# Attention and two mixtures of experts on one core: a new order for the first jobs of the second mixture, with earlier weight stores

## The chip, the cores and the metric

One core of one Trainium2 chip runs the whole program. The metric is device time in microseconds (us) of one execution, as the median of several runs.

## The reference, cut to what matters

```
kv  = einsum('bhsd,bhse->bhde', k, v);  out = einsum('bhsd,bhde->bhse', q, kv)   # q,k,v: 4 x 8 x 576 x 64
x   = out / sqrt(mean(out*out, -1) + 1e-6) * g_norm          # then 2304 rows of 512
p   = probs / (probs.sum(-1) + 1e-9)                         # first mixture, 4 experts, all of them
x1  = sum_e p[:, e] * (relu(x @ w1[e]) @ w2[e])              # 512 -> 1024 -> 512
logits = normed(x1) @ normed(emb).T / tau                    # second mixture, 8 experts
idx = argmax(logits);  gate = softmax(logits)[idx]
y[rows of e] = gate * (relu(x1[rows of e] @ w1b[e]) @ w2b[e])
```

Everything is float32.

## The kernel before, in words

Each float32 operand of a large product is split into a rounded high part and the rest (`split`, L60: the high part on ScalarE at L61, the low part on VectorE at L62), and each product is three TensorE products: high by high, high by low, low by high. The order of work on every engine is written out by hand. An engine executes its instructions in the order in which the Python code issues them, so where a call stands decides what it waits behind.

**Attention and the start.** Per batch and pair of heads, `kv_unit` (L120) forms k'v on TensorE and ScalarE copies it out. `x_unit`, `x_norm` and `xt_unit` (L186, L199, L221) form, normalise and transpose one tile of 128 rows; `x_norm` ends on VectorE at L202 and `xt_unit` transposes on TensorE at L225. The units of batch 1 read their k and v from memory that is later `en_b`.

**First mixture.** The rows go in units of 384. The first two units run four plain phases (`plain_phase`, L1143): four steps of the first layer (`plain_unit`, TensorE at L841), then six steps of the second (`l2_unit`, L948, two for each tile of 128 rows). A list `todo` hands side work out by a modelled time: `run_steps` issues an entry as soon as the sum of the steps' modelled times has passed the entry's. P1T = 8.4 is the end of a plain phase's first layer. The side work is, among other things, `w2_fills` (the split of two blocks of the second layer's weights into `w2h`, `w2l`, L1150), and `hold_now` (L77): it issues the stores that were put off, on the SyncE queue (SP, L69), which copy split weights to DRAM for later passes. Before, `hold_now` stands after all steps of the plain phase. The other units run phases with Strassen's scheme in 14 steps (TensorE at L853, ScalarE and VectorE sums at L860 and L864), with second-layer steps behind them (loop at L1196 on); `w2_fills(e, fh, 1, 6)` at L1200 spreads the two splits of w2 over the modelled times 1 to 6.

**Routing.** The last six tiles (t = 12 to 17) get their logits as products: after the tile's last `l2_unit`, an entry of `due` issues `logits_t` (L341, four transposes at L346, which read the tile `fin` that VectorE writes at L957) two ticks later and `logits_u` (L351) two more ticks on. A tick is one call of `background`, one per step. After the last tile the generator `route_b` (L533) is put into `bg`. It picks experts, counts places (`ranks`, L410, TensorE at L415), and inverts the places into lists of rows for the jobs (`invert`, L450: VectorE makes one-hot tiles `po` at L364, TensorE counts with them into `psi` at L476). `background` advances it by pieces; nearly all of them are small VectorE instructions. The first 12 tiles have been routed earlier (`route_a`), which gives the first NA = 5 jobs of 128 rows.

**Second mixture.** It runs jobs of one expert and 128 rows each. `gather` (L748, GpSimd) fetches a job's rows, `tx_unit` (L1118) transposes them on TensorE and splits them into `xgt` (high on ScalarE at L1123, low on VectorE, tile `xgl`, L360), `m1_unit` (L1234) is half of a first layer (12 steps of TensorE's L1240 per half of F, 24 per job), `th_unit` (L1248) transposes and splits half of its result, `m2_unit` (L1272) is a second layer (24 steps of L1262), `m2_out` (L1264) scales and scatters it. `slot_split` (L783) splits a job's weights; from job 2 on under a condition (`tc.If`, L791), because a job with the expert of two jobs earlier keeps its weights. `period` (L1290) pairs the first layer of job s with the second layer of job s - 1:

```
hn = m1_unit(s, 0), m1_unit(s, 1)
while (s + 2 >= NA and "placed" not in late): background(1)
ps = m2_unit(s - 1, ..., fill = tx_unit(s + 1), gather(s + 2))
th_unit(s, 0), th_unit(s, 1), m2_out(s - 1, ps)
```

For s = 0 there is no second layer, so the order is m1(0), tx_unit(1), th(0), m1(1). `tx_unit(1)` writes the same `xgt` that m1(0) reads. At s = 3 the rows of job 5 are gathered, which is the first gather that needs all of `route_b` (`placed`).

Of the kernel before, what the change touches and what calls it, by code (L numbers as in the profile page):

```python
# [20 lines left out]
def attn_moe_moe_kernel(ctx: ExitStack, tc: tile.TileContext, q, k, v, g_norm, dprobs, w1, w2, emb, tau, w1b, w2b, out):  # L21
    nc = tc.nc
# [277 lines left out]

    def inv_norm(a, shape, tag):
        pool = late.get("tmp", rt_p)
        b, r, y = (pool.tile(shape, F32, name=n, tag=n + tag) for n in ("inb", "inr", "iny"))
        nc.vector.tensor_scalar_max(b, a, 1e-30)
        nc.scalar.activation(out=r, in_=b, func=ACTF.Sqrt)
        twice_root(r, b, y)
        nc.vector.tensor_scalar(out=b, in0=r, scalar1=0.5, scalar2=1e-6, op0=ALU.mult, op1=ALU.add)
        nc.vector.reciprocal(b, b)
        return b

    def setup_emb():
# [29 lines left out]
    def logits_t(t, x):  # L341
        xx = late["tmp"].tile([128, NC, 128], F32, name="xx", tag="xx")
        due.append((tick[0] + (2 if t < NT - 1 else 1), t, lambda: logits_u(t, xx)))
        ps = psp.tile([128, NC, 128], F32, name="pslt", tag=f"x{t % 2}" if t < NT - 1 else nxt("l2"))
# [5 lines left out]

    def logits_u(t, xx):  # L351
        pl = psp.tile([128, E2], F32, name="psl", tag="kv")
        for c in range(NC):
            nc.tensor.matmul(out=pl, lhsT=xx[:, c], rhs=en_t[:, c], start=(c == 0), stop=(c == NC - 1))
        nc.vector.tensor_copy(lg[:, t], pl)
        if t == NT - 1:
            bg.append(route_b())
# [30 lines left out]

    def gate_exp(t0, t1, rx):
        l = lg[:, t0:t1]  # L390
        tt(l, l, bc(rx, [128, t1 - t0, E2], 2), ALU.mult)
        nc.scalar.activation(out=l, in_=l, func=ACTF.Exp)

# [96 lines left out]
    def route_a():  # L490
        rx = inv_norm(ssq[:, 0:TA], [128, TA], "a")
        yield from pick(0, TA)
        gate_exp(0, TA, rx)
        yield 1
# [37 lines left out]

    def route_b():  # L533
        rx = inv_norm(ssq[:, TA:NT], [128, NT - TA], "b")
        yield 0
        yield from pick(TA, NT)
        gate_exp(TA, NT, rx)
        yield 1
        ps, run = ranks(TA, NT)
        yield 0  # L540
        tab = tmp([128, E2], "tab")
        tt(tab, st_a, cnt, ALU.add)
        yield from places(TA, NT, ps, run, tab)
        gate_sum(TA, NT)
# [392 lines left out]
    def l2_unit(t, e, fh, part, i, first):  # L937
# [21 lines left out]
        if last:  # L959
            nc.gpsimd.dma_start(out=x1d[128 * t:128 * t + 128, :], in_=ac)  # L960
            if t < TA:
                bg.append(logits_v(t, ac))
            else:
                due.append((tick[0] + 2, t, lambda: logits_t(t, ac)))
            if t == TA - 1:
# [131 lines left out]
    for t in range(TS):  # L1097
        xt_unit(t, ("tp", "l10", "l11")[t], first=True)
    issue()
    def norm_probs():  # L1100
# [15 lines left out]
    xgt = []  # L1116

    def tx_unit(s):  # L1118
        xg = xgs.pop(s)
        ps = psp.tile([128, NC, 128], F32, name="pstx", tag="tp")  # L1120
        for c in range(NC):
            nc.tensor.transpose(ps[:, c], xg[:, 128 * c:128 * c + 128], ident)  # L1122
        nc.scalar.copy(xgt[0], ps)  # L1123
        tt(xgt[1], ps, xgt[0].bitcast(F32), ALU.subtract)

# [17 lines left out]
    def plain_phase(un, e, fh, todo, pace):  # L1143
        steps = [(P1T / 4, lambda f=f: plain_unit(un % 2, f)) for f in range(4)]
        steps += l2_steps(e, fh, [un], None, first_half, (P2T - P1T) / 6)
        run_steps(steps, todo, pace)
        if un == 0:
            hold_now()

# [13 lines left out]
    todo = w2_fills(0, 0) + [(-1, f) for f in plain_direct(1)]  # L1163
    todo += [(1.5 + 2 * p, lambda p=p: kv_unit(1, p)) for p in range(2, NP)] + [(6.0, norm_probs)]
    todo += [(10.0 + c, lambda c=c: nc.vector.tensor_tensor(
# [30 lines left out]
    for at_ph, ph in enumerate(strassen):  # L1196
        p, e, fh = ph
        steps = [(S1T / 14, f) for f in strassen_steps()]
        steps += l2_steps(e, fh, [2 * p, 2 * p + 1], (0, 1, 2, 0, 1, 3), lambda t: 0, (S2T - S1T) / 12)
        todo = w2_fills(e, fh, 1, 6) + ahead.get(ph, []) + carried + [(8.8, hold_now)]  # L1200
        carried = []
# [32 lines left out]
    def m1_unit(s, half, mid):  # L1234
        xh, xl = xgt
        ps = psp.tile([128, 512], F32, name="psm1", tag=nxt("l1"))
# [44 lines left out]
    def ahead_of(s):  # L1281
        if s + 1 < NS:
            tx_unit(s + 1)
        if s + 2 < NS:
            gather(s + 2)

    def idle():
        pass

    def period(s, mid1, mid2):  # L1290
# [3 lines left out]
        mid1()  # L1294
        while min(s + 2, NS - 1) >= known[0] or (s + 2 >= NA and "placed" not in late):
            background(1)
        if s:
            ps = m2_unit(s - 1, mid2, lambda: ahead_of(s))
        else:
            ahead_of(s)  # L1300
        th_unit(s, 0, hn[0])
        th_unit(s, 1, hn[1])
        if s:
            m2_out(s - 1, ps)

    def full_period(s):
        work2 = [lambda n=n: slot_split("w2", s, [n]) for n in range(4)]
        work1 = [lambda n=n: slot_split("w1", s + 1, [n]) for n in range(4 if s + 1 < NS else 0)]
        if s == 0:
            work1, work2 = work2, []  # L1310

        def side(work):
            if work:
                work.pop(0)()
            background(2 if s + 2 < NA else 1)

# [4 lines left out]

    for s in range(SURE):
        full_period(s)
# [50 lines left out]
```

## Time and profile before

| | |
|---|---|
| median of 3 runs | 1139.51 us (1139.37 to 1140.52) |
| the profiled execution | 1139.33 us |
| its span in the trace | 1137.5 us |
| TensorE busy | 1106.6 us, 97% of the span |
| VectorE busy | 629.6 us, 55% |
| ScalarE busy | 484.9 us, 43% |
| GpSimd busy | 190.1 us, 17% |

The span is the time between the first and the last instruction of the trace; the execution's own time is 1.8 us more. A time in a row is counted from the span's start. In a timeline, a row has the start, the duration, the engine (PE TensorE, ACT ScalarE, DVE VectorE, POOL GpSimd, SPq the issuing of transfers by SyncE), the line of the code, the operation, output<-inputs, shape and count, and in brackets how long the engine stood idle before and what ended that.

### The profile page before, as it was taken

What the parts mean: (1) busy time and instruction counts of PE and PEld (TensorE: products, weight loads), DVE (VectorE), ACT (ScalarE), POOL (GpSimd) and SP (SyncE); (2) the same over time, 40 slices, a digit from 0 to 9 for tenths busy, and PEclk for the clock granted to TensorE, in tenths of its full rate; (3) what the DMA queues carried; (4) which work ended last, traced back from release to release, by engine and by line L of the source; (5) the groups of instructions that cost most, each with busy time, mean ns of one, the idle gap of its engine ahead of it and who ended that gap; (6) DMA issues with size and microseconds to landing.
All of it is one profiled execution on the core that took longest, in us unless ns stands there. A gap on an engine that the chain in (4) does not pass through costs nothing. (4 is left out here: it accounts for less than half of the span.)

```text
span 1137.5 us, 17164 instructions
## 1 busy us (share of the span) xinstructions
PE 1106.6 (97%) x5894; PEld 970.7 (85%) x5894; DVE 629.6 (55%) x1187; ACT 484.9 (43%) x892; POOL 190.1 (17%) x232
## 2 busy tenths in 40 slices
PE   8989999999999999999999999999987999999997
PEld 7878898988888988899999988889876888888885
DVE  3555664666794456544573556643468573376362
ACT  3534446544454222233334222222464574475462
POOL 3101332313441100100120000010110112111211
PEclk9989999999999999999999999999999999999999
DMA  9645777766877455455465555445554583575571
GB/s 269 199 145 210 290 285 291 256 216 265 305 260 266 171 200 192 164 200 204 173 238 192 179 208 213 184 172 199 209 186 142 192 327 118 180 261 216 164 256 35
DMA packets 91011, 239.85 MB, mean 211 GB/s; under 512 B 19285, under 2 KB 38741, under 8 KB 90784
## 3 DMA queue, kind: packets, MB, share of 16 engines
q1 hardware_dynamic: 83472, 214.23, 53.2%
q0 software_dynamic: 7440, 24.41, 6.4%
q8 instruction: 49, 0.80, 0.3%
q14 instruction: 50, 0.41, 0.1%
HBM read 230.22 MB, written 56.63 MB: 252 GB/s over the span
## 5 line engine op out<-in xcount | busy, mean ns | idle before, releaser
L948 PE MATMUL bank<-w2h,hh 128*128 128x512 f32 x576 | 227.4, 395 | 0.2 <-ACT hh L825 0.2
L948 PE MATMUL bank<-w2l,hh 128*128 128x512 f32 x576 | 225.0, 391 | 0.1
L948 PE MATMUL bank<-w2h,hl 128*128 128x512 f32 x576 | 225.1, 391 | 0.0
L853 PE MATMUL bank<-xth,w1h 128*128 128x384 f32 x616 | 159.9, 340 | 2.5 <-ACT s L860 1.1
L853 PE MATMUL bank<-xtl,w1h 128*128 128x384 f32 x616 | 156.8, 335 | 0.0
L853 PE MATMUL bank<-xth,w1l 128*128 128x384 f32 x616 | 156.7, 335 | 0.0
L957 DVE SCALAR_TENSOR_TENSOR acc<-bank,dp,acc 128x512 f32<-128x512 f32 x120 | 89.8, 749 | 110.0 <-PE bank L948 109.8
L948 PEld LDWEIGHTS bank<-w2h,hl 128*128 128x128 f32 x576 | 108.2, 188 | 24.0 <-DVE hl L828 1.1
L948 PEld LDWEIGHTS bank<-w2h,hh 128*128 128x128 f32 x576 | 108.2, 188 | 22.4 <-ACT hh L825 1.4
L948 PEld LDWEIGHTS bank<-w2l,hh 128*128 128x128 f32 x576 | 108.2, 188 | 21.5 <-DMA w2l<-held_w 0.5
L853 PEld LDWEIGHTS bank<-xth,w1h 128*128 128x128 f32 x616 | 109.5, 188 | 6.7 <-ACT s L860 1.6
L62 DVE TENSOR_TENSOR w2l<-raw,w2h 128x1024 fp32r<-128x1024 f32 x64 | 76.7, 1220 | 64.0 <-ACT w2h L61 59.9
L853 PEld LDWEIGHTS bank<-xtl,w1h 128*128 128x128 f32 x616 | 111.5, 188 | 0.0
L853 PEld LDWEIGHTS bank<-xth,w1l 128*128 128x128 f32 x616 | 111.3, 188 | 0.0
L860 ACT COPY s<-bank 128x384 f32<-128x384 f32 x88 | 42.2, 479 | 157.6 <-PE bank L853 157.5
L864 POOL TENSOR_TENSOR sv<-sv,s 128x384 f32<-128x384 f32 x44 | 48.3, 1097 | 350.3 <-ACT sv L860 274.0
L336 DVE CUSTOM_DVE_ANT_0 scr<-row,en_b 128x512 bf16<-128x512 f32 x96 | 68.4, 713 | 13.4 <-DMA row<-x1d 8.6
L1262 PE MATMUL psy<-w2h,hth 128*128 128x512 f32 x176 | 72.2, 410 | 0.4 <-ACT hth L1253 0.4
L1262 PE MATMUL psy<-w2l,hth 128*128 128x512 f32 x176 | 69.8, 396 | 0.0
L1262 PE MATMUL psy<-w2h,htl 128*128 128x512 f32 x176 | 69.4, 394 | 0.0
L61 ACT CAST w2h<-raw 128x1024 fp32r<-128x1024 f32 x64 | 65.7, 1052 | 7.1 <-DMA raw<-in_moe_w_dram 2.8
L62 DVE TENSOR_TENSOR w1l<-raw,w1h 128x256 fp32r<-128x256 f32 (+2 forms) x75 | 55.3, 754 | 16.9 <-ACT w1h L61 16.5
(249 smaller groups left out, 1657.2 us busy)
## 6 DMA issues: line engine op xcount, KB each, us to landing
raw<-in_moe_w_dram SPq DMA_DIRECT2D x224, 512.0 KB
w1h<-held_w SPq DMA_DIRECT2D x28, 896.0 KB
w1l<-held_w SPq DMA_DIRECT2D x28, 896.0 KB
w2h<-held_w SPq DMA_DIRECT2D x34, 512.0 KB
w2l<-held_w SPq DMA_DIRECT2D x34, 512.0 KB
held_w<-w1h SPq DMA_DIRECT2D x16, 896.0 KB
held_w<-w1l SPq DMA_DIRECT2D x16, 896.0 KB
held_w<-w2h SPq DMA_DIRECT2D x16, 512.0 KB
```

Of the source, the lines that this page charges most:

```text
L61: nc.scalar.copy(hi, raw)
L62: (eng or nc.vector).tensor_tensor(out=lo, in0=raw, in1=hi.bitcast(F32), op=ALU.subtract)
L336: nc.vector.tensor_tensor_reduce(out=scr, in0=x, in1=en_b[:, e], scale=1.0, scalar=0.0, op0=ALU.mult, op1=ALU.add, accum_out=lg[:, t, e:e + 1]
L853: nc.tensor.matmul(out=ps, lhsT=wform(wo, b, w)[:, c], rhs=xform(xo, x)[:, c], start=start and n == 0, stop=(n == 5), skip_group_check=True)
L860: nc.scalar.copy(t, src)
L864: (eng or nc.vector).tensor_tensor(out=out, in0=a, in1=b, op=ALU.add)
L948: nc.tensor.matmul(out=ps, lhsT=h_t[o][f][u][:, ns], rhs=w[j][:, a], start=(k == 0 and m == 0), stop=(k == 3 and m == 2))
L957: nc.vector.scalar_tensor_tensor(out=fin, in0=ps, scalar=dp[:, t, e:e + 1], in1=ac, op0=ALU.mult, op1=ALU.add)
L1262: nc.tensor.matmul(out=ps, lhsT=x[:, f], rhs=w[j][:, o], start=(f == 0 and i == 0), stop=(f == NF - 1 and i == 2))
```

## The change

Seven edits. (1) The units of batch 1's pairs 2 and 3 are issued before the first plain phase and not at modelled times inside it. (2) In the plain phases of unit 0, `hold_now` is issued at P1T + 0.05, between the layers. (3) In the last phase of the first pass with Strassen's scheme, (0, 3, 1), the two splits of w2 are spread over 0.1 to 3.0. (4) `logits_t` comes one tick later for tiles 12 to 16; `logits_u` of tile 16 follows after one tick. (5) `inv_norm` is cut in two; in `route_b` its start comes with the last logits, its end and the products with it come after `ranks`, the exponential after that. (6) Job 1's x is split into the memory of the last w2 part of odd jobs, and the order becomes m1(0), m1(1), m2(0), with `tx_unit(1)` and `th_unit(0, ...)` inside the first layers; the weights of jobs 0 to 2 are split at new places; `route_b` goes forward by two pieces a tick in the first period and one from then on. (7) Job 5's gather, and the loop that finishes `route_b`, move behind job 2's second layer; that puts the products of `invert` into period 3, the fourth job.

```diff
@@ -298,15 +298,21 @@
-    def inv_norm(a, shape, tag):
+    def inv_start(a, shape, tag):
         pool = late.get("tmp", rt_p)
         b, r, y = (pool.tile(shape, F32, name=n, tag=n + tag) for n in ("inb", "inr", "iny"))
         nc.vector.tensor_scalar_max(b, a, 1e-30)
         nc.scalar.activation(out=r, in_=b, func=ACTF.Sqrt)
+        return b, r, y
+
+    def inv_end(b, r, y):
         twice_root(r, b, y)
         nc.vector.tensor_scalar(out=b, in0=r, scalar1=0.5, scalar2=1e-6, op0=ALU.mult, op1=ALU.add)
         nc.vector.reciprocal(b, b)
         return b
+
+    def inv_norm(a, shape, tag):
+        return inv_end(*inv_start(a, shape, tag))
@@ -340,7 +346,7 @@
     def logits_t(t, x):
         xx = late["tmp"].tile([128, NC, 128], F32, name="xx", tag="xx")
-        due.append((tick[0] + (2 if t < NT - 1 else 1), t, lambda: logits_u(t, xx)))
+        due.append((tick[0] + (2 if t < NT - 2 else 1), t, lambda: logits_u(t, xx)))
         ps = psp.tile([128, NC, 128], F32, name="pslt", tag=f"x{t % 2}" if t < NT - 1 else nxt("l2"))
         for c in range(NC):
             nc.tensor.transpose(ps[:, c], x[:, 128 * c:128 * c + 128], ident)
@@ -349,6 +355,8 @@
         nc.scalar.activation(out=sq.rearrange("p r n -> p (r n)"), in_=x, func=ACTF.Square, accum_out=ssq[:, t:t + 1])
     def logits_u(t, xx):
+        if t == NT - 1:
+            late["rx"] = inv_start(ssq[:, TA:NT], [128, NT - TA], "b")
         pl = psp.tile([128, E2], F32, name="psl", tag="kv")
         for c in range(NC):
             nc.tensor.matmul(out=pl, lhsT=xx[:, c], rhs=en_t[:, c], start=(c == 0), stop=(c == NC - 1))
@@ -386,9 +394,12 @@
         tt(oh[:, :, s].rearrange("p e t -> p t e"), a, bc(m2, sh, 2), ALU.is_equal)
         yield 1
-    def gate_exp(t0, t1, rx):
+    def gate_mul(t0, t1, rx):
         l = lg[:, t0:t1]
         tt(l, l, bc(rx, [128, t1 - t0, E2], 2), ALU.mult)
+
+    def gate_exp(t0, t1):
+        l = lg[:, t0:t1]
         nc.scalar.activation(out=l, in_=l, func=ACTF.Exp)
     def gate_sum(t0, t1):
@@ -490,7 +501,8 @@
     def route_a():
         rx = inv_norm(ssq[:, 0:TA], [128, TA], "a")
         yield from pick(0, TA)
-        gate_exp(0, TA, rx)
+        gate_mul(0, TA, rx)
+        gate_exp(0, TA)
         yield 1
         ps, run = ranks(0, TA)
         yield 0
@@ -531,15 +543,13 @@
         late["ready"] = True
     def route_b():
-        rx = inv_norm(ssq[:, TA:NT], [128, NT - TA], "b")
-        yield 0
         yield from pick(TA, NT)
-        gate_exp(TA, NT, rx)
-        yield 1
         ps, run = ranks(TA, NT)
+        gate_mul(TA, NT, inv_end(*late["rx"]))
         yield 0
         tab = tmp([128, E2], "tab")
         tt(tab, st_a, cnt, ALU.add)
+        gate_exp(TA, NT)
         yield from places(TA, NT, ps, run, tab)
         gate_sum(TA, NT)
         yield 0
@@ -961,7 +971,7 @@
             if t < TA:
                 bg.append(logits_v(t, ac))
             else:
-                due.append((tick[0] + 2, t, lambda: logits_t(t, ac)))
+                due.append((tick[0] + (3 if t < NT - 1 else 2), t, lambda: logits_t(t, ac)))
             if t == TA - 1:
                 bg.append(route_a())
@@ -1096,6 +1106,8 @@
         nc.vector.tensor_tensor(out=x_s[t], in0=px[t], in1=ri[:, t].unsqueeze(2).to_broadcast([128, H, DH]), op=ALU.mult)
     for t in range(TS):
         xt_unit(t, ("tp", "l10", "l11")[t], first=True)
+    for p in range(2, NP):
+        kv_unit(1, p, ("kv", "l21")[p - 2])
     issue()
@@ -1115,13 +1127,20 @@
     xgt = []
+    x_of = {}
+
     def tx_unit(s):
         xg = xgs.pop(s)
+        if s == 1:
+            x_of[s] = [wb[1][0][3][:, i].rearrange("p (c t) -> p c t", t=128) for i in range(2)]
+        else:
+            x_of[s] = xgt
         ps = psp.tile([128, NC, 128], F32, name="pstx", tag="tp")
         for c in range(NC):
             nc.tensor.transpose(ps[:, c], xg[:, 128 * c:128 * c + 128], ident)
-        nc.scalar.copy(xgt[0], ps)
-        tt(xgt[1], ps, xgt[0].bitcast(F32), ALU.subtract)
+        hi, lo = x_of[s]
+        nc.scalar.copy(hi, ps)
+        tt(lo, ps, hi.bitcast(F32), ALU.subtract)
     P1T, P2T = 8.4, 16.6
     S1T, S2T = 14.7, 31.1
@@ -1143,9 +1162,9 @@
     def plain_phase(un, e, fh, todo, pace):
         steps = [(P1T / 4, lambda f=f: plain_unit(un % 2, f)) for f in range(4)]
         steps += l2_steps(e, fh, [un], None, first_half, (P2T - P1T) / 6)
+        if un == 0:
+            todo = todo + [(P1T + 0.05, hold_now)]
         run_steps(steps, todo, pace)
-        if un == 0:
-            hold_now()
     def w2_fills(e, fh, t0=0, t1=P1T):
         return spread([lambda n=n: fill_w2(e, 2 * fh + n) for n in range(2)], t0, t1)
@@ -1161,7 +1180,7 @@
     xs_f = x_fills()
     w1_blocks(0, 1)
     todo = w2_fills(0, 0) + [(-1, f) for f in plain_direct(1)]
-    todo += [(1.5 + 2 * p, lambda p=p: kv_unit(1, p)) for p in range(2, NP)] + [(6.0, norm_probs)]
+    todo += [(6.0, norm_probs)]
     todo += [(10.0 + c, lambda c=c: nc.vector.tensor_tensor(
         out=xr[:, 0, c], in0=xform(0, 0, 2)[:, c].bitcast(F32), in1=xform(1, 0, 2)[:, c].bitcast(F32), op=ALU.add)) for c in range(NC)]
     plain_phase(0, 0, 0, todo + w1_plain_fills(0, 1) + spread(att([TS]), 4.5, 15.5) + [(16.0, lambda: qt_unit(TS + 1))], [0] * 99)
@@ -1197,7 +1216,7 @@
         p, e, fh = ph
         steps = [(S1T / 14, f) for f in strassen_steps()]
         steps += l2_steps(e, fh, [2 * p, 2 * p + 1], (0, 1, 2, 0, 1, 3), lambda t: 0, (S2T - S1T) / 12)
-        todo = w2_fills(e, fh, 1, 6) + ahead.get(ph, []) + carried + [(8.8, hold_now)]
+        todo = w2_fills(e, fh, *((0.1, 3.0) if ph == (0, E1 - 1, 1) else (1, 6))) + ahead.get(ph, []) + carried + [(8.8, hold_now)]
         carried = []
         if at_ph + 1 < len(strassen):
             p2, e2, f2 = strassen[at_ph + 1]
@@ -1232,7 +1251,7 @@
     hts = [s_p.tile([128, NF, 128], F32R, name=f"ht{n}", bufs=1) for n in "hl"]
     def m1_unit(s, half, mid):
-        xh, xl = xgt
+        xh, xl = x_of[s]
         ps = psp.tile([128, 512], F32, name="psm1", tag=nxt("l1"))
         n = 0
         for c in range(NC):
@@ -1281,45 +1300,87 @@
     def ahead_of(s):
         if s + 1 < NS:
             tx_unit(s + 1)
-        if s + 2 < NS:
+        if s + 2 < NS and s + 2 != NA:
             gather(s + 2)
     def idle():
         pass
+
+    def split_one(kind, s, n):
+        return lambda: slot_split(kind, s, [n])
+
+    def step(work, n=1):
+        background(n)
+        for f in work:
+            f()
+
+    first_h = []
+
+    def first_period():
+        w2_0 = [split_one("w2", 0, n) for n in range(4)]
+        first_h.append(m1_unit(0, 0, lambda: step([lambda: tx_unit(1), lambda: gather(2)])))
+        step(w2_0[:1], 2)
+
+        def mid():
+            th_unit(0, 0, first_h[0])
+            step([], 2)
+
+        first_h.append(m1_unit(0, 1, mid))
+        step(w2_0[1:2], 2)
+
+    def second_period():
+        w2_0 = [split_one("w2", 0, n) for n in range(2, 4)]
+        w1_2 = [split_one("w1", 2, n) for n in range(4)]
+        w2_1 = [split_one("w2", 1, n) for n in range(4)]
+
+        def mid():
+            th_unit(0, 1, first_h[1])
+            step(w2_0[:1])
+
+        hn = [m1_unit(1, 0, mid)]
+        step(w2_0[1:])
+        hn.append(m1_unit(1, 1, lambda: step(w1_2[:1])))
+        step(w1_2[1:2])
+        left = [w1_2[2:3], w1_2[3:] + w2_1[:1], w2_1[1:3], w2_1[3:]]
+        ps = m2_unit(0, lambda: step(left.pop(0)), lambda: ahead_of(1))
+        th_unit(1, 0, hn[0])
+        th_unit(1, 1, hn[1])
+        m2_out(0, ps)
+        background(1)
     def period(s, mid1, mid2):
         hn = [m1_unit(s, 0, mid1)]
         mid1()
         hn.append(m1_unit(s, 1, mid1))
         mid1()
-        while min(s + 2, NS - 1) >= known[0] or (s + 2 >= NA and "placed" not in late):
+        while min(s + 2, NS - 1) >= known[0]:
             background(1)
-        if s:
-            ps = m2_unit(s - 1, mid2, lambda: ahead_of(s))
-        else:
-            ahead_of(s)
+        ps = m2_unit(s - 1, mid2, lambda: ahead_of(s))
         th_unit(s, 0, hn[0])
         th_unit(s, 1, hn[1])
-        if s:
-            m2_out(s - 1, ps)
+        m2_out(s - 1, ps)
+        if s + 2 == NA:
+            while "placed" not in late:
+                background(1)
+            gather(NA)
     def full_period(s):
-        work2 = [lambda n=n: slot_split("w2", s, [n]) for n in range(4)]
-        work1 = [lambda n=n: slot_split("w1", s + 1, [n]) for n in range(4 if s + 1 < NS else 0)]
-        if s == 0:
-            work1, work2 = work2, []
+        work2 = [split_one("w2", s, n) for n in range(4)]
+        work1 = [split_one("w1", s + 1, n) for n in range(4 if s + 1 < NS else 0)]
         def side(work):
             if work:
                 work.pop(0)()
-            background(2 if s + 2 < NA else 1)
+            background(1)
         period(s, lambda: side(work1), lambda: side(work2))
         for split_rest in work1 + work2:
             split_rest()
         background(1)
-    for s in range(SURE):
+    first_period()
+    second_period()
+    for s in range(2, SURE):
         full_period(s)
     n_used = nc.values_load(
         rt_n[0:1, 0:1], engines=[ENG.PE, ENG.Activation, ENG.DVE, ENG.Pool, ENG.SP], min_val=SURE, max_val=NS,
```

## Rows read from the trace of the kernel before

**Rows 1.** The page's first part: busy time of each engine.

```profile
PE 1106.6 (97%) x5894; PEld 970.7 (85%) x5894; DVE 629.6 (55%) x1187; ACT 484.9 (43%) x892; POOL 190.1 (17%) x232
```

**Rows 2.** Waits of TensorE, whole span: waiter, releaser, us in total, times, longest.

```profile
PE psi L476 <- DVE po L364: 5.4, 1, 5.4
PE psxt L225 <- DVE xs L202: 4.5, 2, 4.2
PE psm L1240 <- ACT xgh L1123: 3.6, 1, 3.6
PE pslt L346 <- DVE fin L957: 1.9, 4, 0.6
...
PE bank L853 <- ACT s L860: 1.1, 1, 1.1
...
PE bank L853 <- DVE s L864: 0.5, 1, 0.5
```

**Rows 3.** Timeline of TensorE, the first plain phase.

```profile
26.27 0.94 PE L841 MATMUL bank<-xth,w1h 128*128 128x384 f32 x4 [1.42 <-DVE xtl L233]
...
36.29 0.69 PE L128 MATMUL pskv<-en_b 128*64 128x64 f32 x16
37.16 0.50 PE L948 MATMUL bank<-w2h,hh 128*128 128x512 f32 x1
```

**Rows 4.** Timeline of the issuing of transfers by SyncE.

```profile
20.01 0.44 SPq L140 DMA_DIRECT2D en_b<-in_v_dram  x1
```

**Rows 5.** Timeline of all engines, the second plain phase.

```profile
55.95 1.05 ACT L61 CAST w2h<-raw 128x1024 fp32r<-128x1024 f32 x1 [2.67 <-DMA held_w<-w2h]
...
57.24 1.23 DVE L62 TENSOR_TENSOR w2l<-raw,w2h 128x1024 fp32r<-128x1024 f32 x1 [3.76 <-DMA held_w<-w2l]
```

**Rows 6.** Timelines of TensorE and ScalarE behind that wait.

```profile
60.62 1.09 PE L225 MATMUL psxt<-ident,xs 128*128 128x128 f32 x4 [4.22 <-DVE xs L202]
...
63.45 0.60 ACT L194 ACTIVATE xs<-psx 128x512 f32<-128x512 f32 x1 [1.02 <-PE psx L180]
...
69.48 0.66 PE L225 MATMUL psxt<-ident,xs 128*128 128x128 f32 x4
```

**Rows 7.** Stretches: length, busy time and instructions by engine, PEclk, DMA share, GB/s.

```profile
42.00:46.00 4.00, 3.68 (x20) 2.79 (x19) 3.79 (x11) 2.59 (x6) 0.00 (x0) 1.00 0.00 0
60.00:70.00 10.00, 9.38 (x41) 8.60 (x42) 5.35 (x12) 3.01 (x5) 2.83 (x4) 0.70 0.28 82
848.00:858.00 10.00, 6.70 (x25) 5.44 (x26) 6.64 (x21) 3.49 (x6) 0.00 (x0) 0.83 0.62 184
878.00:888.00 10.00, 9.12 (x43) 6.93 (x44) 4.64 (x21) 0.59 (x1) 0.00 (x0) 0.66 0.14 51
```

**Rows 8.** Timeline of VectorE, phase (0, 3, 1).

```profile
284.61 1.22 DVE L62 TENSOR_TENSOR w2l<-raw,w2h 128x1024 fp32r<-128x1024 f32 x1 [3.88 <-ACT w2h L61]
```

**Rows 9.** TensorE at the first job's and the fourth job's first layer: timeline, chain.

```profile
838.06 0.40 PE L1240 MATMUL psm<-xth,xgh 128*128 128x512 f32 x1
...
888.61 5.67 PE psm L1240 x24
```

**Rows 10.** VectorE in between: two rows of its timeline.

```profile
838.26 0.75 DVE L957 SCALAR_TENSOR_TENSOR fin<-bank,dp,acc 128x512 f32<-128x512 f32 x1 [2.07 <-PE bank L948]
...
878.57 0.57 DVE L364 TENSOR_SCALAR po<-lane_b,pos 128x128 bf16<-128x128 bf16 x3
```

**Rows 11.** Waits of VectorE from 838 to 880 (columns as in rows 2).

```profile
DVE w2l L62 <- ACT w2h L61: 3.3, 1, 3.3
...
DVE run L418 <- PE psr L415: 1.7, 1, 1.7
DVE xgl L360 <- ACT xgh L1123: 0.8, 1, 0.8
```

**Rows 12.** Timeline of ScalarE at a table load.

```profile
843.90 1.28 ACT L305 ACT_TABLE_LOAD   x1
845.33 0.21 ACT L305 ACTIVATE inr<-inb 128x6 f32<-128x6 f32 x1
```

## The prediction

> **What bounds the kernel now.** I read the page first: TensorE is busy for 97% of the span [rows 1], so nothing off its path counts, and what can be won is its waits and the time in which it runs at half its clock. The waits of TensorE give the places [rows 2]: one of 5.4 us for `po` and one of 3.6 for job 1's x in the second mixture, one of 4.2 for the normalised tile in the second plain phase, four short ones before the logits' transposes, two in the Strassen phase (0, 3, 1). The timelines tell who was late, and the stretches tell what follows: behind the three long waits PEclk falls from 1.00 to 0.50 (from 2.4 to 1.2 GHz), which shows as 0.70, 0.83 and 0.66 over the ten us around each [rows 7].
>
> **The change, part by part.** The sum is made against the profiled execution, 1139.33 us, 0.2 below the median of 1139.51.
>
> *Units of pairs 2 and 3 (edit 1).* One unit takes TensorE from 36.29 to 37.16, 0.87 us; two leave the first phase, 1.75. They go into a gap: TensorE stands idle for 1.42 us until 26.27, waiting for VectorE [rows 3]. They overrun it by 0.33 if their k and v are there. The last of these was issued at 20.45 [rows 4]; by bytes (6.55 MB are asked for up to it) I put its landing at 25.8, just at the second unit, and allow 0.2 more. Bounds: no wait, gain 1.4; landing 1.5 late, gain 0. I take **1.2**. The ScalarE copies behind them fall into that engine's idle time; if it were not idle, they would cost their 0.4 each.
>
> *Stores at half phase (edit 2).* The next split writes the tiles that the stores read, so ScalarE stands 2.67 us and VectorE 3.76 us until they have read [rows 5]; `x_norm` is queued behind that split on VectorE, and TensorE waits 4.22 us for it, to 60.62 [rows 6]. Their data is there when the second layer starts to read it, at 37.16 [rows 3], and from 42 to 46 hardly a transfer runs [rows 7], so issued at half phase they meet no load; the loads queued behind them on SyncE slip by four issues, and no TensorE wait in rows 2 is for a load of weights. Without the wait ScalarE's cast starts 2.67 earlier, and so does the whole chain: the transposes at 57.95, still 1.55 late, since the split itself stands ahead of `x_norm`. I take it that this shorter wait leaves the clock at its upper level. The next transposes come 6.03 us after ScalarE reads the tile (63.45 to 69.48) [rows 6]. Transposes and products ahead of that read took 60.62 to 63.45, 2.83 at half clock, and take 1.42 at full; so 57.95 + 1.42 + 6.03 = 65.4 in place of 69.48: **4.0** gained. Bounds: 2.7 if the half clock stays, 6.7 if both left waits vanish. What is late next is the split, then `x_norm`. In the phase after it SyncE issues the stores as soon as the split is done already; nothing there.
>
> *Splits of w2 in (0, 3, 1) (edit 3).* VectorE idles 3.88 us before the first of the two splits, 1.22 each [rows 8], and is crowded afterwards, where TensorE waits 0.5 and 1.1 [rows 2]. Two steps earlier the splits fall into the idle time and shorten the crowd by about 1.2. Bounds 0 and 1.6; I take **1.1**.
>
> *Logits a tick later (edit 4).* The four waits are 1.9 in all, 0.6 the longest [rows 2]; a tick there is six products, at 0.236 each [rows 9] 1.4 us. All go: **1.9**, bounds 1.0 and 1.9.
>
> *The first jobs (edits 5 to 7).* Removed are the waits for job 1's x, 3.6, and for `po`, 5.4: 9.0. PEclk of 0.83 and 0.66 over ten us is 3.4 and 6.8 us at half clock; less the idle ends, half of each is lost: 1.5 and 3.0, so 13.5 together. But VectorE is what was late, and its work is only put elsewhere. Its ledger: from the last `fin` to the first `po` 838.26 to 878.57, 40.3 us [rows 10], of which it waited 3.3 + 1.7 + 0.8 [rows 11]; 34.5 of work and short gaps. The new order asks nearly the same before job 3's x is split (two one-hot products go behind it, one split of x comes ahead): 34.2, ready 34.4 after 838.06. TensorE gets there after 888.61 - 838.06 = 50.55 [rows 9] less 13.5 less the 18 counting products (0.8 by their columns at the rate of rows 9, 4.2 by count; 1.6 taken, nearer to the columns): 35.4. So without any VectorE wait TensorE waits for nothing; with 5.8 as before for 4.8. In the new order VectorE still waits at the start (for the logits' products, and for x behind ScalarE's copy and square); I take 5.3, and split the lateness into about 1.2 at job 2's x and 3.4 at job 3's. The second is near the 3.6 of before, so I add that one's 1.5 at half clock. 13.5 - 4.6 - 1.5 = **7.4** gained; bounds 0 (all waits come back) and 13.5. The counting products cost the same in the fourth job; each group's `po` is made a tick ahead. GpSimd's gather of job 5 now stands behind job 2's scatter; its transposes come a first layer (5.67 [rows 9]) and half a second one later, which covers it. SyncE's loads keep their order.
>
> The activation tables are loaded twice in this stage, as before; ScalarE's load took 1.28 us and the next activation began 0.15 after its end [rows 12]. The Trainium skill (ScalarE: Activation LUTs, What ACT_TABLE_LOAD costs) charges a drain of 1.38 us on top; by it the sum would be 2.8 worse, 12.8 gained. The row shows no such drain; I keep 1.28.
>
> Sum: 1.2 + 4.0 + 1.1 + 1.9 + 7.4 = 15.6; 1139.3 - 15.6 = 1123.7, and 0.2 for the median: **1123.9 us**. This case's own range is 1119.5 to 1128.5.
>
> **The rivals.** *VectorE's backlog keeps its whole price*: TensorE waits at jobs 2 and 3 as long as before, at half clock after it. For it: VectorE is within a us of TensorE's pace even without waits. Against it: its first 10 us have idle time that the new order fills. Gain 8.2: 1131.3.
>
> *VectorE keeps up*: no wait is left in the first jobs. For it: 34.4 against 35.4. Against it: the 5.8 us of waits. Gain 8.2 + 13.5 = 21.7: 1117.8.
>
> *The stores don't move*: SyncE's queue still holds them behind loads that wait for a free buffer, so that the split waits as before. Against it: those loads are issued after the phase's half. Gain 11.6: 1127.9.
>
> *The table loads cost double*: at their new places ScalarE's two loads stand ahead of the first two splits of job 0's second layer, and VectorE waits for those casts. If each load held ScalarE for twice its 1.28, VectorE would be 2.6 later at job 3: 1126.5. The 0.15 of rows 12 speaks against it. The rule of the Trainium skill's page named above works this way.
>
> *Slower*: in the fourth job TensorE meets five groups of counting products inside job 2's second layer, and in order each waits for its `po`, which VectorE makes behind that job's splits of w2. If each waits 5.4 as the one of before did [rows 2], 27 us are lost against 15.6 won: 1139.5 - 15.6 + 27 = 1150.9. It decides from 3.1 us a group on. Against it: one split is 1.22 us, and a group has a tick's lead.
>
> *No effect*: the issue order binds in another place than the code's text says, and all waits stay: 1139.5.
>
> **How the numbers follow.** Chances: forecast 0.59, backlog 0.17, keeps up 0.10, stores 0.05, table loads 0.03, slower 0.03, no effect 0.03. The range 1118 to 1131.5 takes in the forecast's own, the stores, the table loads, the backlog to a little above its value and the near part of the case in which VectorE keeps up; about 2 in 10 stay outside. A measurement can tell 0.2%, 2.3 us, from no change. All cases but the last two lie over 2.3 below: faster 0.94, same 0.03, slower 0.03.
>
> **What would show it.** In the changed kernel's trace: first-layer products from about 26.5 on with both units ahead of them; no release by `held_w` in the second plain phase, and a wait of about 1.5 there for `xs` with PEclk at 1.00; no wait of `pslt` for `fin`; no wait of `psi` for `po` of more than half a us; instead waits of `psm` for VectorE's `xgl` at jobs 2 and 3, 4 to 5 us in sum. The prediction is wrong if `psm` waits there for over 8 us or not at all, if `psi` waits in the fourth job, if the units of pairs 2 and 3 wait for their transfers, or if a new wait appears in the phases behind the first two.

## The result and the profile after

The changed kernel took 1122.86 us (median of 4 runs, 1122.72 to 1123.65) against 1139.44 of the kernel before beside it: a ratio of 0.9855, 95% interval 0.9838 to 0.9872, 16.6 us saved. The prediction was 1123.9, range 1118.0 to 1131.5. The profiled executions differ by 15.6 us in their spans (1137.5 and 1121.9), and the working below is read against these. Of the kernel with the shared memory below, one execution of six took 6249.93 us; its median of 1123.1 counts that one, and the other five have 1122.85.

The page's first line for TensorE, which answers to [rows 1]. Its busy time fell by only 4.2 us; the rest of the gain is idle time:

```profile
PE 1102.4 (98%) x5894; PEld 967.9 (86%) x5894; DVE 630.4 (56%) x1187; ACT 484.8 (43%) x892; POOL 192.9 (17%) x232
```

Waits of TensorE in the changed kernel from 800 to 900 us (columns as in [rows 2]):

```profile
PE psm L1259 <- DVEq L801: 3.3, 1, 3.3
PE psm L1259 <- DVE xgl L368: 1.3, 1, 1.3
PE psi L487 <- DVE po L372: 0.2, 1, 0.2
```

and from 0 to 110 us:

```profile
PE psxt L225 <- DVE xs L202: 1.9, 3, 1.2
PE psq L163 <- DMA xr<-in_q_dram: 1.5, 1, 1.5
```

Of [rows 2], `po` went from 5.4 to 0.2, `xs` from 4.5 to 1.9, and the four waits of `pslt` and the wait for job 1's `xgh` are gone. In their place stand two new ones, 4.6 us, for jobs 2 and 3.

TensorE in the two plain phases, by its timeline (answers to [rows 3, 6]):

```profile
25.70 0.69 PE L128 MATMUL pskv<-en_b 128*64 128x64 f32 x16
26.78 0.69 PE L128 MATMUL pskv<-en_b 128*64 128x64 f32 x16
27.65 0.97 PE L851 MATMUL bank<-xth,w1h 128*128 128x384 f32 x4
...
56.92 0.63 PE L225 MATMUL psxt<-ident,xs 128*128 128x128 f32 x4 [1.23 <-DVE xs L202]
...
64.55 0.66 PE L225 MATMUL psxt<-ident,xs 128*128 128x128 f32 x4 [0.36 <-DVE xs L202]
```

Both units of pairs now stand ahead of the first layer. What stood at 60.62 and 69.48 stands at 56.92 and 64.55. SyncE and ScalarE tell why (their timelines):

```profile
38.02 0.46 SPq L69 DMA_DIRECT2D held_w<-w2h  x1
...
41.25 0.92 SPq L69 DMA_DIRECT2D held_w<-w2l  x1
```

```profile
52.48 1.03 ACT L61 CAST w2h<-raw 128x1024 fp32r<-128x1024 f32 x1
```

The stores are issued around 38 to 42 us, and the cast that stood 2.67 us for them [rows 5] starts at 52.48 with no wait.

The first jobs, by TensorE's timeline:

```profile
828.37 0.47 PE L1259 MATMUL psm<-xth,xgh 128*128 128x512 f32 x1
...
852.20 0.50 PE L1259 MATMUL psm<-xth,xgl 128*128 128x512 f32 x1 [1.28 <-DVE xgl L368]
...
868.34 0.79 PE L1259 MATMUL psm<-w1h,xgl 128*128 128x512 f32 x1 [3.30 <-DVEq L801]
...
874.05 0.52 PE L1259 MATMUL psm<-w1h,xgh 128*128 128x512 f32 x1
...
885.00 0.48 PE L1259 MATMUL psm<-xth,xgh 128*128 128x512 f32 x1
```

The releaser of the long wait, `DVEq`, is VectorE's sequencer at a branch; what the product reads is the `xgl` that ends just before it (VectorE's timeline):

```profile
867.61 0.68 DVE L368 TENSOR_TENSOR xgl<-pstx,xgh 128x512 fp32r<-128x512 f32 x1
```

After it 13 products take 868.34 to 874.05, 5.7 us where 13 at 0.233 take 3.0: half clock. The stretches say the same (columns as in [rows 7]); where [rows 7] have 0.70 from 60 to 70 there is 1.00 now, and the half clock behind job 3's x remains:

```profile
60.00:70.00 10.00, 9.28 (x42) 6.99 (x41) 6.96 (x12) 3.72 (x6) 3.07 (x3) 1.00 0.62 224
...
858.00:868.00 10.00, 7.04 (x37) 5.56 (x36) 9.43 (x23) 4.99 (x9) 2.24 (x3) 0.98 0.18 62
868.00:878.00 10.00, 9.66 (x36) 7.38 (x36) 4.78 (x17) 1.54 (x3) 0.00 (x0) 0.68 0.74 251
```

VectorE is busy 9.43 of the ten us before job 3's x is there: it sets the pace. The gain by place: the first job's first product moved from 838.06 [rows 9] to 828.37, 9.7 earlier; the fifth job's (job 4) from the row below, in the timeline of the kernel before, to 885.00, 15.9 earlier. So the stretch of the first jobs, from the first job's first product to the fifth job's, fell from 62.8 to 56.6: the first jobs gave 6.2. From there on the two kernels run alike.

```profile
900.88 0.48 PE L1240 MATMUL psm<-xth,xgh 128*128 128x512 f32 x1
```

### The profile page after: what moved, and what is told of

It reads as the page before. It is cut to its first block, busy times and chain, and to the rows that moved or that the text cites. A ratio compares the mean times of both kernels' runs of the same rounds, so it can differ in the third digit from the quotient of the medians.

```text
span 1121.9 us, 17162 instructions
## 1 busy us (share of the span) xinstructions
PE 1102.4 (98%) x5894; PEld 967.9 (86%) x5894; DVE 630.4 (56%) x1187; ACT 484.8 (43%) x892; POOL 192.9 (17%) x232
```

## The experiments

Theory: each of the edits 1 to 4 took away the wait it was charged with, and in the first jobs the order lets TensorE work while VectorE catches up, so that its lateness is paid once, at job 3's x. Rivals: the gain of the first jobs came from VectorE's shorter waits alone (edit 5), from the counting moved to the fourth job (edit 7), or from the own memory of job 1's x (two of the expectations below call it job 2's x, counting from one). Each kernel is the changed one with one edit, and each was run against the kernel before; "left out" means set back to what it was.

**Edit 2 left out.**

```diff
-        if un == 0:
-            todo = todo + [(P1T + 0.05, hold_now)]
         run_steps(steps, todo, pace)
+        if un == 0:
+            hold_now()
```

> The changed kernel with edit 2 undone: the stores stand behind the plain phase again. Theory (the place of the stores makes the split wait, and TensorE behind it): the 4.1 us that the second plain phase won are lost, 1127.0 us; VectorE's split is released by held_w again, TensorE waits some 4 us for xs there and PEclk falls to 0.50 behind it. Rival (the wait would be small anyway, now that the first phase is shorter): 1122.9 to 1124.

Measured: 1125.21 us, 0.9873 (0.9858 to 0.9888), 2.4 over the changed kernel. Its waits of TensorE from 0 to 110 us and the stretch after it:

```profile
PE psxt L225 <- DVE xs L202: 4.4, 2, 4.0
```

```profile
60.00:70.00 10.00, 10.00 (x45) 8.97 (x43) 4.73 (x10) 3.94 (x7) 2.83 (x4) 0.75 0.28 86
868.00:878.00 10.00, 6.70 (x36) 4.90 (x35) 8.19 (x23) 2.33 (x5) 1.09 (x1) 1.00 0.53 192
```

The wait and the half clock behind it are back, and the second plain phase takes 4.1 longer: that was edit 2. The whole lost less than was expected: 2.4 by the medians, and only 0.8 by the profiled executions (1124.47 and 1123.65). In these 2.7 came back at job 3: TensorE waits 3.3 there too, but PEclk reads 1.00 afterwards.

**Edit 1 left out.** The two units go back into the first phase:

```diff
-    for p in range(2, NP):
-        kv_unit(1, p, ("kv", "l21")[p - 2])
...
+    todo += [(1.5 + 2 * p, lambda p=p: kv_unit(1, p)) for p in range(2, NP)]
```

> The changed kernel with edit 1 undone: the units of pairs 2 and 3 inside the first plain phase again. Theory (they fill TensorE's gap): 1.6 us slower by the trace of the changed kernel, 1124.5; by the prediction's own term 1.2, 1124.1. Rival (ahead of the phase they only wait for their transfers): 1122.9.

Measured: 1123.4 us, 0.9857 (0.9842 to 0.9872). Its waits of TensorE from 0 to 110 us, and the stretch behind job 3's wait:

```profile
PE bank L851 <- DVE xtl L233: 1.4, 1, 1.4
```

```profile
868.00:878.00 10.00, 8.66 (x36) 6.51 (x36) 5.63 (x18) 1.73 (x3) 0.21 (x1) 0.83 0.70 249
```

The gap is back and costs 1.6 up to the second phase; 1.2 of it is won back because the half clock lasts 3.4 us at job 3 where the changed kernel's trace has 6.8. The total cannot be told from the changed kernel's.

**Edit 3 left out.**

```diff
-w2_fills(e, fh, *((0.1, 3.0) if ph == (0, E1 - 1, 1) else (1, 6)))
+w2_fills(e, fh, 1, 6)
```

> The changed kernel with edit 3 undone: the splits of w2 in phase (0, 3, 1) at the modelled times 1 to 6 again. Theory (the splits crowd VectorE): 2.2 us slower by the trace of the changed kernel, 1125.1; by the prediction's term 1.1, 1124.0; TensorE waits for s and for a sum of VectorE there again. Rival (the waits went because everything comes at other times): 1122.9.

Measured: 1125.03 us, 0.9873 (0.9859 to 0.9888). Its profiled execution, 1122.42, is not slower than the changed kernel's, since no half clock follows job 3's wait in it; so the place itself is read. Waits of TensorE from 280 to 330 us, in this kernel:

```profile
PE bank L863 <- DVE acc L967: 1.1, 2, 1.0
PE bank L863 <- ACT s L870: 1.1, 1, 1.1
PE bank L863 <- DVE s L874: 0.5, 1, 0.5
```

and in the changed one:

```profile
...
PE bank L863 <- DVE acc L967: 0.3, 1, 0.3
```

The two waits of [rows 2] come back, and one for `acc` grows. The place loses 2.2 already ahead of the phase's second layer: the first layer takes 16.77 us here and 14.57 in the changed kernel. The wait for `acc` comes half a phase later and is not in the 2.2; the two waits for `s`, 1.65 by their rows, make all of it. TensorE's timeline shows how:

```profile
286.20 0.51 PE L863 MATMUL bank<-xtl,w1h 128*128 128x384 f32 x2
287.24 0.62 PE L863 MATMUL bank<-xth,w1h 128*128 128x384 f32 x2 [0.52 <-DVE s L874]
287.70 0.51 PE L863 MATMUL bank<-xth,w1l 128*128 128x384 f32 x2
```

A row lasts 0.51, but without a wait the next one begins 0.35 after it: the rows overlap by 0.16, and the idle time in brackets is counted from the end of the row before. So a wait of 0.52 puts 1.04 between two starts in place of 0.35, and another 0.46 pass up to the start of the row after it. That is 0.8 lost for a wait of 0.5; the other wait, 1.13, costs 1.4 in the same way.

**Edit 4 left out.**

```diff
-            due.append((tick[0] + (3 if t < NT - 1 else 2), t, ...))
+            due.append((tick[0] + 2, t, ...))
```

(and `NT - 2` in `logits_t` is `NT - 1` again)

> The changed kernel with edit 4 undone: the logits' transposes two ticks after the tile's last product again. Theory (they wait for the tile): the four waits come back, 1.9 us by the prediction, 2.6 by the landmarks of the two traces: 1124.8 to 1125.5. Rival (VectorE is late in the first jobs, so that what TensorE loses ahead of them is won back as a shorter wait there): 1122.9 to 1123.5.

Measured: 1125.96 us, 0.9877 (0.9862 to 0.9891), 3.1 over the changed kernel. Waits of TensorE from 790 to 830 us:

```profile
PE pslt L352 <- DVE fin L967: 1.6, 3, 0.6
```

The waits are back (a fourth, of 0.30, stands at 830.90, behind this window): 1.9 by the rows, as before. The place loses 2.6, for the reason seen at edit 3. Around the first of the four waits the products on both sides begin 1.15 apart (811.52 and 812.67) in place of 0.59 (811.13 and 811.72): 0.56 lost for a wait of 0.36.

**The order of the first jobs left out (edit 6).** Each job's own first layer, transposes and second layer come again in the order of before; job 1's x keeps its memory, edits 5 and 7 stay.

```diff
-    first_period()
-    second_period()
-    for s in range(2, SURE):
+    for s in range(SURE):
         full_period(s)
```

(with the branches for job 0 in `period` and `full_period` as in the kernel before, and with them its places of the weight splits and its two pieces of `route_b` a tick up to the third job)

> The first two jobs in the order of the kernel before (first layer, first layer's transposes, then the next job), everything else as in the changed kernel: job 2's x in its own memory, the root and exponential at their new places, the gather of the fourth job's table behind the third job. Theory: the order is what lets TensorE work while VectorE catches up, so most of the 6.2 us that the first jobs won goes again: TensorE waits 4 to 6 us at the first layers of jobs 2 and 3 instead of 4.8 in sum with 10 us of products more ahead of them; time 1126 to 1129 us. Rival (VectorE's shorter list alone, that is edit 5, won it): waits as in the changed kernel, time within 1 us of 1122.9.

Measured: 1129.32 us, 0.9912 (0.9898 to 0.9925), 6.5 over the changed kernel (5.0 by the profiled executions) and a little above what was expected. Waits of TensorE from 840 to 900 us:

```profile
PE psi L487 <- DVE po L372: 3.2, 2, 2.2
PE psm L1259 <- ACT w2h L1142: 2.3, 1, 2.3
PE psm L1259 <- DVE xgl L368: 2.2, 1, 2.2
```

7.7 us of waits where the changed kernel has 4.8, for the x of jobs 1 and 2 and at the counting. The stretch of the first jobs takes 61.5 us, where it was 62.8 before and is 56.6 in the changed kernel: 4.9 of the 6.2 are gone. Edits 5, 7 and the memory are all in this kernel, so none of them makes the gain by itself. The order, the places of the splits and the pace of the routing were set back together, and which of the three counts was not tested.

**The root and the exponential left out (edit 5)**: they stand where they stood, the new order stays.

```diff
 def route_b():
+    rx = inv_norm(ssq[:, TA:NT], [128, NT - TA], "b")
     yield from pick(TA, NT)
+    gate_mul(TA, NT, rx)
+    gate_exp(TA, NT)
     ps, run = ranks(TA, NT)
-    gate_mul(TA, NT, inv_end(*late["rx"]))
```

> The square root and the exponential of the second routing back where the kernel before has them; the order of the jobs and all else as in the changed kernel. Theory (VectorE's list sets when job 3's x is there): VectorE stands again for ScalarE's table load, root and exponential, up to the 5.8 us that it stood there in the kernel before, of which 2 to 4 reach job 3's x: TensorE waits 5 to 7 us there instead of 3.3, and the time is 1125 to 1127 us. Rival (the backlog of the gather and of the weight splits sets it, the waits for ScalarE run beside): the wait stays 3.3 us and the time within 1 us of 1122.9.

Measured: 1127.48 us, 0.9891 (0.9876 to 0.9906), 4.6 over the changed kernel. Waits of TensorE from 840 to 900 us:

```profile
PE psm L1260 <- DVEq L802: 4.8, 1, 4.8
PE psi L485 <- DVE po L370: 2.1, 3, 1.1
```

VectorE's list matters as well: job 3's x comes 1.5 later against TensorE, and then the counting products wait for `po`. The stretch of the first jobs takes 60.0 us: 3.3 of the 6.2 are lost there. Another 1.6 had gone ahead of it in the profiled run, most of it between 47 and 307 us, where this edit touches nothing.

**Both left out.**

> Both at once: the first two jobs in the order of the kernel before, and the second routing's root and exponential at their old places; job 2's x in its own memory and the late gather stay. The old order alone gave 1129.3 us and the old root alone 1127.5 us, 6.4 and 4.6 us over the changed kernel. Theory A (one chain: either part wins nothing while the other stands in the old way): 1128.5 to 1130.5 us, the two losses don't add. Theory B (each takes its own piece out of VectorE's and TensorE's waits): the losses add, 1132 to 1135 us.

Measured: 1129.8 us, 0.9908 (0.9892 to 0.9925), in the range of theory A: the losses don't add. The waits of TensorE from 840 to 900 us:

```profile
PE psi L485 <- DVE po L370: 5.4, 1, 5.4
PE psm L1260 <- ACT w2h L1143: 3.6, 1, 3.6
```

These are the two waits of [rows 2] to the tenth (`w2h` of L1143 is the high part of job 1's x, named by its new memory), though the late gather and the memory are still in. The stretch takes 62.9 us, as before: without edits 5 and 6 nothing of the 6.2 is left, and edit 7 and the memory win nothing that shows by themselves. Left out one at a time they lose 4.9 and 3.3 by the traces, each with the same 6.8 us at half clock as the changed kernel, and both 6.3: each loss is measured with the other edit in place, and part of it is the same.

What either wins alone, which theory A puts at nothing, is not settled. Against this kernel the new order alone has 2.9 by the traces (62.9 to 60.0) and 2.3 by the medians, the shorter list alone 1.4 and 0.5. But this trace has 13.6 us at half clock in the stretch, and those two 6.8, and the last section shows that the half clock behind one and the same wait can differ by as much. So edits 5 and 6 together make the gain of the first jobs, and neither makes the whole of it alone. That the order gives VectorE time and the shorter list makes that time enough fits this, but it was not shown apart from it.

**Job 5's gather early again (edit 7).**

```diff
-        while min(s + 2, NS - 1) >= known[0]:
+        while min(s + 2, NS - 1) >= known[0] or (s + 2 >= NA and "placed" not in late):
             background(1)
```

(and the gather back in `ahead_of`, its loop behind `m2_out` removed)

> The changed kernel with edit 7 undone: job 5's gather, and the loop that finishes the routing, ahead of job 2's second layer in the fourth job. Theory (by then VectorE has nearly done its list, so the counting products lack only the last pieces): psi waits for po 1 to 2 us in all, 1124 to 1125. Rival (the place of the counting products is what the gain hangs on): the 5.4 us wait and its half clock come back, 1131.

Measured: 1122.15 us, 0.9847 (0.9834 to 0.986): no loss, so the expectation falls. The counting products run ahead of the third job's second layer without a wait (TensorE's timeline):

```profile
872.42 0.35 PE L487 MATMUL psi<-rhs,po 128*128 128x100 bf16 x4
874.08 1.73 PE L487 MATMUL psi<-rhs,po 128*128 128x100 bf16 x14
```

In the new order VectorE has made `po` by then. No half clock follows job 3's wait in this trace, and the stretch of the first jobs takes 53.9 us, as it does in the two other kernels where none follows (without edit 2 and without edit 3): moving the counting out of the third job's way wins nothing.

**Job 1's x in the shared memory again.**

```diff
-        if s == 1:
-            x_of[s] = [wb[1][0][3][:, i].rearrange("p (c t) -> p c t", t=128) for i in range(2)]
-        else:
-            x_of[s] = xgt
+        x_of[s] = xgt
```

(and `tx_unit(1)` and `gather(2)` behind both halves of the first job's first layer)

> The changed kernel with job 1's x in the same memory as job 0's again; its transposes therefore stand behind both first layers of job 0, ahead of job 1's. Theory (in the first jobs VectorE sets the pace, so a wait at job 1 comes off the waits at jobs 2 and 3): a new wait of 3 to 4 us at job 1's x, and 1.3 + 3.3 shrink by most of that; 1122 to 1125. Rival (the waits add): 3.6 and its half clock 1.5 on top, 1128.

Measured: 1123.1 us, 0.9854 (0.984 to 0.9867). Waits of TensorE from 826 to 850 us and, of those from 840 to 900, the longest:

```profile
PE psm L1256 <- ACT xgh L1139: 0.3, 1, 0.3
```

```profile
PE psm L1256 <- DVEq L801: 3.3, 1, 3.3
```

The wait of 3 to 4 us at job 1's x, on which the theory and its rival rest, did not come: it is 0.3, so the run decides between neither. The wait at job 3 is the same 3.3. The stretch of the first jobs takes 56.0 us, and 55.4 in the two kernels with as long a half clock (without edit 1 and without edit 4): the memory wins some 0.6 there, nothing that the totals show.

**Some of VectorE's list put off.** Part of the products that build `rhs`, one operand of the counting, goes behind job 3's x (`side` takes the number of pieces):

```diff
-        period(s, lambda: side(work1), lambda: side(work2))
+        period(s, lambda: side(work1, 2 if s == 3 else 1), lambda: side(work2, 0 if s == 2 else 1))
```

> The changed kernel with VectorE's one-hot products moved: no piece of the routing inside job 1's second layer, two pieces a tick in the fourth job's first layer. Theory (TensorE waits at job 3's x because VectorE gets to its split late): the split of job 3's x comes 1.2 to 2 us earlier, the wait of 3.3 us falls to 1.3 to 2.1 and, if that is short enough, PEclk stays at 1.00: 1118.1 us; if the clock falls all the same, 1121.1. Rival (the wait is for a branch, which the profile names as the releaser, and not for the work ahead of it): 1122.9.

Measured: 1122.19 us, 0.9837 (0.9823 to 0.9851). Waits of TensorE from 840 to 900 us:

```profile
PE psm L1259 <- DVEq L801: 2.5, 1, 2.5
...
PE psi L487 <- DVE po L372: 0.6, 2, 0.5
```

0.8 came off the wait, 0.4 went back to `po`. The wait follows VectorE's list, but less than was forecast, and the stretch of the first jobs takes 55.8 us, not less than the 55.4 of the kernels with as long a half clock (PEclk 0.83 here too).

**TensorE kept busy under the wait.** Twelve products of the identity, whose result nobody reads, ahead of job 3's first layer:

```diff
         th_unit(s, 1, hn[1])
+        if s == 2:
+            keep_warm(12, "kv")
         m2_out(s - 1, ps)
```

> The changed kernel with 12 products of the identity with itself, into a bank that nobody reads, before job 3's first layer, about 2.9 us of work where TensorE waits 3.3. Theory (the wait costs once by itself and once more by the half clock that it leaves behind, 3.0 us): the clock stays at 1.00, the wait at job 3 is under 0.8 us, 1119.9 us. Rival (the half clock has another cause, or costs nothing because VectorE is behind anyway): 1122.9, or more by what the products add.

Measured: 1120.27 us, 0.9832 (0.9818 to 0.9845). TensorE's timeline:

```profile
863.29 2.84 PE L1037 MATMUL warm<-ident 128*128 128x128 f32 x24
...
867.21 0.50 PE L1259 MATMUL psm<-w1h,xgl 128*128 128x512 f32 x1 [0.61 <-DVEq L801]
867.55 0.39 PE L1259 MATMUL psm<-w1h,xgh 128*128 128x512 f32 x1
867.78 0.39 PE L1259 MATMUL psm<-w1l,xgh 128*128 128x512 f32 x1
```

(each product is two records). The x comes no earlier, but the products after it are 0.23 apart instead of 0.43: 2.6 us less than the changed kernel, the 2.7 that its 13 products lost. All ten executions of this kernel and of the next have a mean granted clock of 0.998 or 0.999, the four of the changed kernel 0.996 or 0.997, so a chance is an unlikely reason. This is the fastest version run.

**That and the early gather together.**

> The two experiments that were fastest, joined: twelve products kept under job 3's wait, and the loop that asks for the fourth job's places ahead of the third job's second layer. Theory: they touch different stretches, so their gains add: no half clock after job 3's wait (3.0 us in the changed kernel's profile) and no wait for places and counts in the fourth job; 1118.5 to 1119.8 us. Rival: the earlier counting only moves VectorE's work in front of job 3's weights, then it stays at the 1120.3 of the twelve products alone or above.

Measured: 1121.42 us, 0.9844 (0.9831 to 0.9858). It is not under the twelve products alone, so the expectation falls: the gains don't add. The stretch of the first jobs takes 53.8 us with the twelve products alone and 53.9 with both, as it did with the early gather alone, whose trace had met full clock without them: the early gather has nothing of its own to add.

## Why the prediction was right

The forecast case came out, 1.0 us under its number. By its steps:

- **Units (edit 1).** Forecast 1.2; 1.6 by the experiment's own phase. The first layer started at 27.65, not at 26.5: a wait of 1.5 us for `xr`, a load of q, stands ahead of it in this execution, and the last experiment, with 0.3 there, starts it at 26.75.
- **Stores (edit 2).** Forecast 4.0, wait left 1.55, full clock; 4.1 to 4.2, 1.23 and 1.00.
- **Splits (edit 3).** Forecast 1.1, 2.2 measured. The bound of 1.6 was the sum of the two waits in rows, and it was too low: by the timelines each of the two costs TensorE 0.3 more than its row says.
- **Logits (edit 4).** Forecast 1.9, with bounds to 1.9; 2.6 measured. The upper bound was the sum of the four waits again; here each cost 0.2 more than its row.
- **First jobs (edits 5 to 7).** Forecast 7.4; 6.2. The waits came as said: 1.2 and 3.4 forecast, 1.28 and 3.30 measured, and no `psi` wait over 0.19. The mis-sized term is the half clock behind job 3's x: 1.5 was taken because the wait resembled the 3.6 of before, 2.7 were lost. The ledger of VectorE held. Job 3's x was to be ready 39.7 after the first job's first product (34.4 and 5.3 of waits) and was after 39.9, with waits at the two places that the prediction named, the logits' products and ScalarE's copy of job 1's x, and 1.0 behind casts of ScalarE. By this ledger the lateness is 4.3 (39.7 less 35.4), though, and not the 4.6 that the sum used, and its split between jobs 2 and 3 was taken without a working; that both waits came out to the tenth is partly luck. The gain was charged to "edits 5 to 7" as one: edit 7 wins nothing and the memory 0.6 at most; 5 and 6 make it, and neither makes the whole alone.

The two longest waits of VectorE in the changed kernel from 828 us to job 3's x (`w2h` of L1142 is job 1's x, by its memory):

```profile
DVE lg L363 <- PE psl L362: 2.5, 1, 2.5
DVE w2h L368 <- ACT w2h L1142: 2.1, 1, 2.1
```

Of the rivals, the kernel comes near the backlog at its whole price (1131.3) when the order is left out (1129.3), and none of the others came. The table loads cost what was taken, as ScalarE's timeline of the changed kernel shows:

```profile
833.77 1.28 ACT L305 ACT_TABLE_LOAD   x1
835.07 0.21 ACT L305 ACTIVATE inr<-inb 128x6 f32<-128x6 f32 x1
```

The load begins 0.01 after the end of the activation ahead of it (833.76), and the next activation begins 0.02 after the load's end. The Trainium skill (ScalarE: Activation LUTs, What ACT_TABLE_LOAD costs) has a drain of 1.38 us besides; the trace does not agree with it here.

The sum was nearer than its terms, which is luck: 1.2 too much for the jobs stands against 2.3 too little for edits 1 to 4 (10.5 by phases against 8.2), and 0.9 lost at the start.

## What to carry to other kernels

Where an engine's list is as long as the critical engine's own work, an order that puts independent work of the critical engine first and a shorter list for the late engine can be one measure: here both were needed for the 6.2 us. Try both before judging either. When a wait of a few us on TensorE can't be removed, look at the products behind it: with the clock at half they can cost nearly as much again (2.7 behind a wait of 3.3), and a few idle products under the wait gave 2.6 us here. Price a wait by how far apart the products on both sides of it begin, and not by its idle row: where products overlap, each short wait here cost 0.2 to 0.3 us more than its row says, and two upper bounds failed by that.

## What had not been expected of the hardware

The same wait at the same place is followed by different stretches at half clock. TensorE waits 3.3 us for job 3's x in the changed kernel and in the kernels without edits 1, 2, 3, 4, 7 and without the new memory; in the profiled executions the half clock behind it lasted 6.8 us (changed kernel), 3.4 (edits 1, 4, memory) and 0 (edits 2, 3, 7), which PEclk from 868 to 878 shows as 0.68, 0.83 and 1.00. The stretch of the first jobs goes with it: 56.6 us with 6.8 at half clock, 55.4 without edit 1 or 4, 53.9 without edit 2, 3 or 7. This moves a total by up to 2.7 us and makes the leave-one-out times of 1 or 2 us uncertain; so the phases were read, not only the totals. What decides between the three was not settled: all have busy TensorE ahead of the wait.
